# Sliding-window attention with a channel mix on one core: how batch 0's q and k come in, the bias matmuls, and the order of all five engines

## The chip, the core and the metric

The kernel runs on one core of a Trainium2 chip. A core has five engines with an instruction stream each: PE (TensorE, matmul), DVE (VectorE), ACT (ScalarE), POOL (GpSimd) and SP (SyncE, here only a queue of DMA issues). They work on SBUF and PSUM memory with 128 partitions and wait for each other on semaphores. DMAs are issued by SP and by POOL; in this kernel, POOL's also convert fp32 in DRAM to bf16 on the way, SP's don't. The metric is the device time of one execution in microseconds (us), as the median of several runs.

## What is computed

Inputs are q, k, v of 8 batches, 8 heads, 576 positions and head size 64, all fp32. The attention looks back over a window of 128 positions with a linear bias per head; its output, with the heads side by side (512 columns), is the input of a channel mix with a hidden size of 1024.

```
scores = scale * np.matmul(q, k.transpose(0, 1, 3, 2))
bias = slopes[:, None, None] * (-np.abs(rel).astype(np.float32))[None, :, :]
mask = (rel >= 0) & (rel < window)          # window = 128
scores = np.where(mask, scores + bias[None], -1000000000.0)
attn = softmax(scores)
x = matmul(attn, v)                         # heads side by side: [8, 576, 512]
x_prev = x shifted by one position
xk = mu_k * x + (1.0 - mu_k) * x_prev
xr = mu_r * x + (1.0 - mu_r) * x_prev
k = np.maximum(xk @ w_k, 0.0)
v = k * k @ w_v
r = 1.0 / (1.0 + np.exp(-(xr @ w_r)))
out = r * v
```

## The kernel before

**Tiles and stages.** The work of the attention is cut into 32 items: item `it` is batch `it // 4` and the pair `it % 4` of heads. The channel mix runs over 4 pairs of batches P (1152 rows), each cut into chunks of rows that begin at c0; `fo` counts the 8 blocks of the hidden size, and `c` the blocks of 128 rows of a pair. Every step is an op with a name, an engine, an estimate of its time and what it depends on:

- `lq`, `lql`, `lqp`, `lqn`: loads of q and k. `lq.g.i` (SP, `load_qk`, lines 111 to 114) brings fp32 of batch 0, pair g, i=0 for q and 1 for k. `lql.b.w.i` (POOL, `load_ql`, 136 to 140) brings half of the heads w of batch b as bf16. `lqp` (POOL, `load_qp`) does so for pair 1 of batch 0. `lqn.b.i.j` (POOL) brings batches 5 to 7 in another layout.
- `lts.b.i`: the last 64 positions ("tail") of q or k; `lvs.b.j`: block j of V; `lwk`, `lwr`, `lwv`: weights; all on POOL.
- `c.g.i`: cast of fp32 to bf16 with positions sorted (`cast_qk`); `ct.it`: the sorting copy alone for data that is bf16 already (`by_token`, DVE).
- `tq`, `tk`: 128x128 transposes of q and k on PE (`qk_transp`); `pq`, `pk`: copies of them from PSUM to SBUF (`qk_copy`). `tail.b`, `tcopy.b`: the same for the tails.
- `score.it.e`: half e of the scores of an item (`scores`, 196 to 230). For the items of batch 0 (`early`) it begins with two matmuls of 512 columns that write bias and mask into PSUM (lines 204 to 210). `exp.it.e`: the exponential on ACT; `mask.it.e`: multiplication with the mask on DVE for the other batches.
- `av.it`: attention times V; `norm.it`: division by the sum (DVE); `ot.it` and `xt.it`: transpose of the result and its copy; from item 12 on `xt` is a transposing DMA on SP. `xk.it`, `xr.it`: the two mixes (DVE).
- `m1` (and `m1a`, its first part for two blocks): xk times w_k; `rl`: relu on ACT; `kk`: its square; `m3`: xr times w_r; `rs`: tanh on ACT; `m2a`, `m2`: the two halves of kk times w_v; `oo`: the product (DVE); `st`: the store (SP).
- `tr.b.i`, `trt.b.i`: transposing DMAs on SP for q, k and tails of batches 5, 6, 7; `fill`, and `warm(8)` at the start: matmuls on zeros. `clear0`, `clear`, `ms`: memsets on POOL that V and `av` need.

**Where batch 0's q and k come from before.** Pair 0 comes as fp32 by two SP loads into the last `qt_buf` and is cast on DVE (`NHW = 1`). Pair 1 comes by two POOL loads (`lqp`), pairs 2 and 3 by two POOL loads (`lql.0.1.*`), as bf16, each followed by one `ct` per pair.

**What sets the order.** `plan()` (480 to 532) issues the ops, but the dictionary `ORDER` (743 to 888) gives, for each engine, the complete list, and each op waits until the one ahead of it in its list has been issued. So an engine executes its list strictly in turn: an op that waits holds up all that stand behind it on that engine. Buffers go around in rings: 2 PSUM buffers "sa" for scores (and `av` from batch 1 on), 4 PSUM buffers "mm" for everything else on PE, 3 "rl", 3 "ct" and so on; an op that takes a new buffer waits until the users of the one that is that many turns back are done.

**Which engine does what.** The engine of a `kk` is set by `KFO` and `KCH` (line 55): blocks 1 and 5 of eight chunks go to ACT (16 squares), the other 88 that are listed to DVE. `pq` and `xt` run on ACT, `pk`, `tcopy` and `c` on DVE.

Of the kernel before, what the change touches and what calls it, by code (L numbers as in the profile page):

```python
# [8 lines left out]
FP32 = mybir.dt.float32  # L9
# [7 lines left out]
def kernel(  # L17
# [59 lines left out]
    ldr = qt_buf[-1].rearrange("p i j g c -> p (i j g c)").bitcast(FP32)[  # L77
        :, 0:4 * NHW * NF * D].rearrange("p (i g h c) -> p i g h c", i=2, g=NHW, h=2)
# [32 lines left out]
    def load_qk(g, i):  # L111
        nc.sync.dma_start(
            out=ldr[:, i, g],
            in_=(q, k)[i][0, 2 * g:2 * g + 2, 0:SM].rearrange("h (p r) d -> p h (r d)", p=128))
# [47 lines left out]
    def qk_transp(it, t0, t1):  # L162
        cs = T["cs", it]
# [19 lines left out]
    def tail_copy(b):  # L183
        t4 = T.pop(("tt", b))[:, 0:128 * G].rearrange("p (g t c) -> p g t c", g=G, t=2)
        nc.vector.tensor_copy(out=tt_buf[b % 2][:, :, 0:3:2], in_=t4)
# [9 lines left out]

    def scores(it, e):
# [5 lines left out]
        w = sum(n for _, _, n in pieces)  # L202
        sa = T["sa", it, e] = p_sa.tile([128, 2, 512], FP32, tag="sa", name="sa")
        if early:
            for hl in range(2):
                nc.tensor.matmul(
                    sa[:, hl, 0:w] if e else sa[:, hl, 0:w].rearrange("p (u c) -> p u c", u=2),
                    lhsT=sid[:, 2 * g + hl],
                    rhs=dist if e else dist[:, None, 0:256].to_broadcast([128, 2, 256]),
                    start=True, stop=False, skip_group_check=True)  # L210
# [74 lines left out]
    def x_copy(it, c0=0, c1=S):  # L285
        b, g = divmod(it, G)
        nc.scalar.copy(out=xt_buf[b % 2][:, g, XO + c0:XO + c1], in_=T.pop(("xt", it, c0))[:, c0:c1])  # L287

    def x_scaled(it, c0, c1):
        if c0 == 0:  # L290
            T["xm", it] = mxp.tile([128, S], BF16, tag="xm", name="xm", bufs=3)
        nc.scalar.activation(out=T["xm", it][:, c0:c1], in_=xt_buf[0][:, it, XO + c0:XO + c1],
                             func=AF.Identity, scale=mu_sb[:, it:it + 1])
# [164 lines left out]
    def clear_first():  # L458
# [3 lines left out]
    RINGS = {"sa": 2, "mm": 4, "ct": 3, "xu": 3, "dl": 4, "xm": 3, "xk": 2, "rl": 3,  # L462
             "kk": 2, "rs": 6, "ot": 4}
# [567 lines left out]
```

## Time and profile before

| | us |
|---|---|
| median of 3 runs | 231.31 (231.19 to 232.16) |
| span of the profiled execution | 230.5 |
| PE busy | 222.2 |
| DVE busy | 192.2 |
| ACT busy | 155.4 |
| POOL busy | 88.7 |

The profiled execution is one run; its span goes from its first to its last instruction. Busy shares are averages over stages with different limits: the same engine can be the limit in the first 40 us and have time to spare later. Matmuls are pipelined, so that a busy PE need not be at its peak: a group of matmuls is better judged by the time until the next group begins, which the chain of work shows. How full the engines are along the span, the page shows in 40 slices of 5.8 us, a digit per slice, in tenths:

```profile
PE   7889899999999999999999999899999999999994
DVE  7577999999998998999798996996876998985252
ACT  4299999985999998783789555685168744226700
```

The DMA queues of the page:

```profile
q0 software_dynamic: 83600, 16.52, 92.3%
q1 hardware_dynamic: 33680, 16.79, 34.1%
```

q0 are the DMAs that POOL issues, q1 those of SP: packets, MB, and the time that their packets took as a share of 16 engines' span.

### The profile page before, as it was taken

To read this page: it belongs to the slowest core of one execution; us is meant where nothing else is said; L and a number is where in the kernel's file an instruction comes from. 1 tells how busy PE (TensorE), PEld (TensorE's weight loads), DVE (VectorE), ACT (ScalarE), POOL (GpSimd) and SP (SyncE) were. 2 spreads that over 40 slices of the span, in tenths; PEclk is the share of its full clock that TensorE was granted. 3 is DMA by queue.
4 is the path that set the end of the run, shared out by engine and by line. 5 is a ranking of instruction groups with operands and counts; after the bars stand their busy time and mean duration, and the time that the engine had idled before them with its cause. 6 is when DMAs were issued, how large, how long until landed. Compare 5 with 4: busy or idle time off the path is not lost.

```text
span 230.5 us, 5326 instructions
## 1 busy us (share of the span) xinstructions
PE 222.2 (96%) x2099; PEld 130.0 (56%) x2099; DVE 192.2 (83%) x409; ACT 155.4 (67%) x265; POOL 88.7 (38%) x127
## 2 busy tenths in 40 slices
PE   7889899999999999999999999899999999999994
PEld 2446577855685565456657554455574555456653
DVE  7577999999998998999798996996876998985252
ACT  4299999985999998783789555685168744226700
POOL 8987857563897000697001954540000000000000
PEclk9999999999999999999999999999999999999999
DMA  6999999999999986999996999999954252413014
GB/s 137 160 173 187 198 177 192 195 180 162 177 155 161 154 120 100 123 128 204 120 256 144 166 120 156 203 176 197 134 128 119 79 163 77 102 46 141 0 67 162
DMA packets 117305, 33.65 MB, mean 146 GB/s; under 512 B 99608, under 2 KB 112928, under 8 KB 117280
## 3 DMA queue, kind: packets, MB, share of 16 engines
q0 software_dynamic: 83600, 16.52, 92.3%
q1 hardware_dynamic: 33680, 16.79, 34.1%
q8 instruction: 16, 0.26, 0.4%
q14 instruction: 9, 0.07, 0.1%
HBM read 33.56 MB, written 9.44 MB: 187 GB/s over the span
## 4 chain that ended last, share of the span: by engine, by line
PE 84%; ACT 7%; DMA 4%; DVE 2%; issue 1%; SPq 0%; DVEq 0%
PE pv L364 25%; PE ps L326 25%; PE pr L349 13%; PE sa L262 7%; PE sa L229 6%; DMA tt<-ts 4%; PE wm L190 3%; PE tp L166 3%; ACT at L237 3%; ACT qk L146 2%; PE pv L371 2%; ACT xt L287 1%; PE tp L282 1%; DVE qk L143 1%; ACT rl L332 1%
## 5 line engine op out<-in xcount | busy, mean ns | idle before, releaser
L237 ACT ACTIVATE at<-sa 128x1024 bf16<-128x1024 f32 x64 | 64.7, 1043 | 14.3 <-PE sa L229 14.2
L326 PE MATMUL ps<-xk,wk_sb 128*128 128x256 bf16 (+2 forms) x416 | 73.2, 314 | 0.5 <-DVE xk L315 0.4
L332 ACT ACTIVATE rl<-ps 128x256 bf16<-128x256 f32 (+2 forms) x104 | 46.3, 482 | 37.0 <-PE ps L326 30.0
L364 PE MATMUL pv<-wv_sb,kk 128*128 128x512 bf16 x272 | 65.3, 379 | 0.0
L326 PEld LDWEIGHTS <-wk_sb 128*128 128x128 bf16 x416 | 38.5, 98 | 24.1 <-issue 2.4
L364 PEld LDWEIGHTS <-kk 128*128 128x128 bf16 x272 | 25.5, 98 | 28.4 <-issue 1.3
L246 DVE TENSOR_TENSOR at<-at,mask 128x1024 bf16<-128x1024 bf16 x56 | 37.4, 684 | 1.9 <-ACT at L237 1.9
L118 POOL DMA_DIRECT2D vs<-in_v_dram x32 | 28.5, 897 | 26.3 <-PE sa L262 16.1
L341 DVE TENSOR_TENSOR kk<-rl 128x256 bf16<-128x256 bf16 (+2 forms) x88 | 28.0, 335 | 10.3 <-ACT rl L332 10.1
L349 PE MATMUL pr<-wr_sb,xr 128*128 128x512 bf16 x144 | 36.0, 379 | 0.0
L379 DVE SCALAR_TENSOR_TENSOR ot<-rs,pv 128x512 f32<-128x512 bf16 (+1 forms) x38 | 24.4, 653 | 7.4 <-PE pv L364 5.8
L315 DVE SCALAR_TENSOR_TENSOR xk<-dl,mu_sb,xt 128x576 bf16<-128x576 bf16 (+2 forms) x36 | 27.1, 752 | 1.3
L315 DVE SCALAR_TENSOR_TENSOR xr<-dl,mu_sb,xt 128x576 bf16<-128x576 bf16 x32 | 25.5, 812 | 0.0
L355 ACT ACTIVATE rs<-pr 128x512 bf16<-128x512 f32 x36 | 21.5, 608 | 4.9 <-PE pr L349 4.6
L262 PEld LDWEIGHTS <-at 128*128 128x128 bf16 x576 | 21.6, 98 | 5.3 <-issue 0.4
L274 DVE TENSOR_TENSOR xu<-sa,rc 128x640 bf16<-128x640 f32 x28 | 23.1, 824 | 1.2 <-DMA xt<-xu 0.3
L146 ACT COPY qk<-tp 128x1024 bf16<-128x1024 bf16 (+1 forms) x20 | 18.9, 960 | 5.6 <-PE tp L166 4.6
L349 PEld LDWEIGHTS <-xr 128*128 128x128 bf16 x144 | 13.2, 98 | 12.6 <-issue 0.4
L90 POOL DMA_DIRECT2D ql<-in_k_dram x12 | 10.9, 919 | 23.0 <-DVE ct L157 21.1
L262 PE MATMUL sa<-vs,at 128*128 128x65 bf16 x448 | 18.9, 194 | 0.0
L308 DVE TENSOR_TENSOR dl<-xt 128x576 bf16<-128x576 bf16 (+2 forms) x36 | 15.1, 420 | 3.2 <-DMA xt<-xu 2.1
L229 PE MATMUL sa<-qk 64*128 64x256 bf16 (+1 forms) x160 | 13.2, 259 | 0.8 <-ACT qk L146 0.5
(70 smaller groups left out, 207.6 us busy)
## 6 DMA issues: line engine op xcount, KB each, us to landing
out_dram<-ot SPq DMA_DIRECT2D x34, 256.0 KB, 3.6
vs<-in_v_dram POOLq DMA_DIRECT2D x32, 128.0 KB, 8.0
ql<-in_k_dram POOLq DMA_DIRECT2D x9, 256.0 KB, 6.7
ql<-in_q_dram POOLq DMA_DIRECT2D x9, 256.0 KB, 7.3
ql<-in_k_dram POOLq DMA_DIRECT2D x13, 128.0 KB, 6.5
ql<-in_q_dram POOLq DMA_DIRECT2D x13, 128.0 KB, 7.6
wk_sb<-in_moe_w_k_dram POOLq DMA_DIRECT2D x2, 512.0 KB, 9.0
wv_sb<-in_moe_w_v_dram POOLq DMA_DIRECT2D x2, 512.0 KB, 8.5
```

The source lines that it names most:

```text
L118: nc.gpsimd.dma_start(out=vs_buf[b % NLD][:, j, :, 0:D], in_=v[b, :, 128 * j:128 * j + 128, :].rearrange("h p d -> p h d"))
L229: nc.tensor.matmul(to, lhsT=kk_, rhs=qq_, start=not early, stop=True, skip_group_check=True)
L237: nc.scalar.activation(out=at_half(it, e), in_=T.pop(("sa", it, e)), func=AF.Exp, scale=float(scale))
L246: nc.vector.tensor_tensor(out=at, in0=at, in1=m, op=ALU.mult)
L262: nc.tensor.matmul(pa[:, hl, W * (t - t0):W * (t - t0) + W], lhsT=at[:, lo:lo + 128], rhs=vs[:, u, 2 * g + hl, :] if u < NF else tvb[:, 2 ...
L315: nc.vector.scalar_tensor_tensor(out=to, in0=T["dl", it][:, c0:c1], scalar=mu_sb[:, NPO * which + g:NPO * which + g + 1], in1=xp, op0=ALU. ...
L326: nc.tensor.matmul(ps[:, 0:c1 - c0], lhsT=wk_sb[:, po, 128 * fo:128 * fo + 128], rhs=xk[:, po, c0:c1], start=(po == 0), stop=(po == NPO - 1))
L332: nc.scalar.activation(out=rl[:, 0:c1 - c0], in_=T.pop(("ps", P, c0, fo))[:, 0:c1 - c0], func=AF.Relu, scale=RELU_SCALE)
L341: nc.vector.tensor_tensor(out=T["kk", P, c0][:, fo, 0:c1 - c0], in0=rl[:, 0:c1 - c0], in1=rl[:, 0:c1 - c0], op=ALU.mult)
L349: nc.tensor.matmul(pr, lhsT=T["xr", P][:, po, 128 * c:128 * c + 128], rhs=wr_sb[:, po], start=(po == 0), stop=(po == NPO - 1))
L364: nc.tensor.matmul(pv, lhsT=kk[:, fo, o:o + 128], rhs=wv_sb[:, fo], start=(fo == 0), stop=(fo == NFO - 1))
L379: nc.vector.scalar_tensor_tensor(out=T["ot", P, c][:, w0:w1], in0=T["rs", P, c][:, w0:w1], scalar=1.0, in1=pv[:, 0:w1 - w0], op0=ALU.add, ...
```

## The change

1. **Loads.** `NHW = 4`: all four pairs of batch 0 come as plain fp32 by SP (eight `lq`), into both `qt_buf` (`ldr` is now a list over the two). `lqp` and `lql.0.*` are gone. The casts `c.g.i` write into `ql_buf[0]` (`cs0`), in the sorted order, so batch 0 has no `ct`. q and k of each pair have their own transposes `tq` and `tk` and their own copies `pq` and `pk`. `lql.2.*` now waits for the transposes of the pairs whose place it takes.
2. **Bias matmuls.** `scores` loses its first two matmuls for the early items; they are an op of their own, `bias.it.e`, which takes the "sa" buffer and depends on nothing but dist and sid.
3. **Engine by list.** `flex` makes an op that runs where the lists of `ORDER` put it, on ACT or on DVE: casts, `pq`, `pk`, `tcopy`, `xt` and, through `ENGOF`, `kk`. By the new lists 41 `kk` run on ACT (16 before); two of eight casts, `pk.0` and three `tcopy` on ACT; `pq.1`, `pq.2`, `pq.5` and `xt.8` on DVE.
4. **Order.** New lists for all five engines. `FILL` is (2, 2) instead of (5, 2, 3).
5. Code that no list used is removed (`XMUL`, `x_scaled`, rings "xm", "xk", "kk").

```diff
-    KFO, KCH = (1, 5), ((0, 512), (0, 768), (1, 0), (1, 512), (1, 896), (2, 0), (2, 512), (2, 896))
-    XMUL = ()
-    NHW = 1
+    NHW = 4
...
-    ldr = qt_buf[-1].rearrange("p i j g c -> p (i j g c)").bitcast(FP32)[
-        :, 0:4 * NHW * NF * D].rearrange("p (i g h c) -> p i g h c", i=2, g=NHW, h=2)
+    ldr = [t.rearrange("p i j g c -> p (i j g c)").bitcast(FP32).rearrange(
+        "p (g i h c) -> p g i h c", g=2, i=2, h=2) for t in qt_buf]
+    cs0 = ql_buf[0].rearrange("p w i h c -> p (w i h c)").rearrange(
+        "p (g i r h d) -> p g i r h d", g=G, i=2, r=NF, h=2)
...
     def cast_qk(g, i, f):
-        if i == 0:
-            T["cs", g] = csp.tile([128, 2, NF, 2, D], BF16, tag="ct", name="cs")
-        f(T["cs", g][:, i].rearrange("p r h d -> p h r d"),
-          ldr[:, i, g].rearrange("p h (r d) -> p h r d", d=D))
+        f(cs0[:, g, i].rearrange("p r h d -> p h r d"),
+          ldr[g // 2][:, g % 2, i].rearrange("p h (r d) -> p h r d", d=D))
...
+    def bias(it, e):
+        g = it % G
+        sa = T["sa", it, e] = p_sa.tile([128, 2, 512], FP32, tag="sa", name="sa")
+        for hl in range(2):
+            nc.tensor.matmul(
+                sa[:, hl] if e else sa[:, hl].rearrange("p (u c) -> p u c", u=2),
+                lhsT=sid[:, 2 * g + hl],
+                rhs=dist if e else dist[:, None, 0:256].to_broadcast([128, 2, 256]),
+                start=True, stop=False, skip_group_check=True)
...
     def square(P, c0, c1, fo):
         rl = T.pop(("rl", P, c0, fo))
-        if fo in KFO and (P, c0) in KCH:
+        if ENGOF.get(("kk", P, c0, fo)) == "ACT":
...
+    def flex(name, eng, busy, run, deps=(), pri=0, alloc=None, uses=()):
+        eng = ENGOF.get(name, eng)
+        f = {"ACT": act_cast, "DVE": vec_cast}[eng]
+        return op(name, eng, busy, lambda: run(f), deps, pri, alloc, uses)
...
+            if early:
+                op(("bias", it, h), "PE", 440, lambda h=h: bias(it, h), [("dcopy",), ("sid",)], n, "sa")
...
-    FILL = (5, 2, 3)
+    FILL = (2, 2)
```

The beginnings of the lists, before and after, as far as the prediction speaks of them ("..." where ops are left out):

```
PE before   fill.0 fill.2 tq.0 fill.1 tk.0 score.0.0 tmu tq.2 tq.3 score.2.0 score.3.0 tail.0
            tq.1 av.0.0 av.2.0 score.2.1 av.3.0 score.0.1 ... score.5.1 m1a.0.0.0 ot.1.1
            ot.3.1 m1.0.0.0 score.7.0 score.7.1 m1.0.0.7 ...
PE after    bias.0.0 tk.0 bias.3.0 tq.0 tk.3 tq.3 score.0.0 tq.2 score.3.0 tk.2 tail.0 fill.1
            bias.2.0 tk.1 score.2.0 tq.1 bias.1.0 av.0.0 av.3.0 tmu score.1.0 bias.2.1 ...
            ot.1.1 fill.0 m1a.0.0.0 m1.0.0.0 m1a.0.0.1 m1.0.0.1 tq.5 score.6.1 score.6.0 ...
ACT before  mask0.2 mask0.0 pq.0 exp.0.0 pq.2 mask0.4 pq.3 exp.2.0 exp.3.0 pq.1 mask0.6 exp.2.1
            exp.0.1 xt.2.0 xt.0.0 exp.1.0 xt.3.0 pq.4 exp.1.1 pq.5 exp.4.0 xt.1.0 exp.3.1 xt.0.1
            xt.2.1 exp.5.0 pq.7 exp.5.1 xt.1.1 xt.3.1 rl.0.0.0 ...
ACT after   mask0.2 mask0.6 mask0.0 mask0.4 c.2.1 pk.0 pq.0 pq.3 exp.0.0 exp.3.0 c.1.0 tcopy.0
            exp.2.0 exp.1.0 xt.0.0 exp.2.1 xt.3.0 xt.2.0 exp.0.1 pq.4 exp.3.1 xt.1.0 exp.1.1
            xt.2.1 xt.0.1 exp.4.0 pq.7 xt.3.1 pq.6 exp.7.0 xt.1.1 exp.4.1 rl.0.0.0 ...
DVE before  dcopy c.0.0 id8 c.0.1 sid pk.0 ct.2 ct.3 pk.2 cmu pk.3 ct.1 tcopy.0 pk.1 norm.2.0 ...
DVE after   id8 dcopy sid c.0.1 c.3.1 mcopy.1 c.0.0 c.3.0 mcopy.0 c.2.0 pk.3 c.1.1 pq.2 pk.2
            pk.1 pq.1 norm.0.0 norm.3.0 cmu norm.2.0 ...
POOL before lql.0.1.1 lql.0.1.0 clear0 lqp.1.1 lvs.0.0 lts.0.1 lqp.1.0 lts.0.0 lvs.0.1 lql.1.0.1
            ms lql.1.0.0 ... lwk.0 lwk.1 ... lqn.5.1.0 lqn.6.1.2 lqn.6.1.1 lvs.4.4 ... lqn.6.0.2
            lvs.5.1 lvs.5.2 lvs.5.0 lvs.5.3 lvs.7.1 ...
POOL after  clear lwk.1 lts.0.1 lts.0.0 ms clear0 lvs.0.0 lvs.0.1 lvs.0.4 lql.1.0.1 lql.1.0.0
            ... lts.1.0 lwk.0 ... lts.6.1 lqn.5.0.0 ... lts.5.1 lqn.6.0.0 lqn.5.1.3 lvs.5.4
            lqn.5.1.1 lts.6.0 lqn.6.1.0 lts.5.0 lqn.5.1.0 lvs.4.0 ... lqn.6.1.3 lvs.7.4 lvs.7.1
            lvs.5.2 lqn.6.0.2 lvs.5.0 lqn.6.0.1 lvs.5.1 ...
SP before   lq.0.0 lq.0.1 lmu.1 lmu.0 st.0.0 ... tr.6.1 tr.6.0 xt.17 ... xt.20 trt.6.0 trt.6.1 ...
SP after    lq.0.0 lq.0.1 lq.3.1 lq.2.1 lq.3.0 lq.2.0 lq.1.1 lq.1.0 lmu.1 lmu.0 st.0.0 ...
            tr.6.1 xt.16 st.0.6 trt.6.1 ... xt.18 st.1.0 trt.6.0 tr.6.0 xt.21 ...
```

The new PE list from the av of item 18 to the first scores of batch 6:

```
av.18 m2a.1.0 m2a.1.2 score.20.1 score.22.1 m2a.1.3 m2.1.0 score.22.0 score.23.0 m2.1.3 m2.1.2
m1.1.512.4 m1.1.512.2 m1.1.896.0 m3.1.4 m1.1.896.6 m3.1.5 m3.1.7 m1.1.512.5 m1.1.512.3 m1.1.896.1
m1.1.512.6 m1.1.512.7 m1.1.896.7 m1.1.896.2 m3.1.6 av.21 m1.1.896.4 m2a.1.6 m1.1.896.5 score.25.1
```

More of the change, by code (lines that the diff above doesn't have):

```diff
@@ L201, in scores @@
         a0 = BASE[pieces[0][0]] + pieces[0][1] - 128 * pieces[0][0]
-        w = sum(n for _, _, n in pieces)
-        sa = T["sa", it, e] = p_sa.tile([128, 2, 512], FP32, tag="sa", name="sa")
         if early:
[L205 to L210, printed above, removed]
+            sa = T["sa", it, e]
+        else:
+            sa = T["sa", it, e] = p_sa.tile([128, 2, 512], FP32, tag="sa", name="sa")
         for (u, q0, n) in pieces:
@@ L605, in add_pair @@
         for h in range(2):
-            op(("score", it, h), "PE", 760 if early else 330, lambda h=h: scores(it, h),
-               ready + (([("trt", b, 0), ("trt", b, 1)] if b in CROSSED else [("tcopy", b), ("clear0",)]) if h else []) + AVOF(it - NAT),
-               n, "sa")
+            if early:
+                op(("bias", it, h), "PE", 440, lambda h=h: bias(it, h), [("dcopy",), ("sid",)], n, "sa")
+            held = [("bias", it, h)] if early else []
+            op(("score", it, h), "PE", 330, lambda h=h: scores(it, h),
+               ready + (([("trt", b, 0), ("trt", b, 1)] if b in CROSSED else
+                         [("tcopy", b), ("clear0",)]) if h else []) + AVOF(it - NAT),
+               n, None if early else "sa", uses=held)
             op(("exp", it, h), "ACT", 920, lambda h=h: expo(it, h),
-               [], n, uses=[("score", it, h)])
+               [("score", it, h)], n, uses=[("bias" if early else "score", it, h)])
             got.append(("exp", it, h))
@@ L924, in add_qk @@
                [("tr", b - 2, 0), ("tr", b - 2, 1)] if b - 2 in CROSSED else
-               [("ct", G * (b - 2) + 2 * w + j) for j in range(2)]
-               if b > 2 or b == 2 and w else [], dma=dma[i], land=min(b, 2) * 700)
+               [("ct", G * (b - 2) + 2 * w + j) for j in range(2)] if b > 2 else
+               [(t, g) for t in ("tq", "tk") for g in range(2 * w, 2 * w + 2)] if b == 2 else [],
+               dma=dma[i], land=min(b, 2) * 700)
     def add_tails(b):
```

421 lines of the change are left out of this document (192 added, 229 removed).

## The prediction

> **What bounds the kernel now.** I read the page's busy line and slices first, then the table of stretches, then the order of time in the opening, then the waits.
>
> ```profile
> span 230.5 us, 5326 instructions
> PE 222.2 (96%) x2099; PEld 130.0 (56%) x2099; DVE 192.2 (83%) x409; ACT 155.4 (67%) x265; POOL 88.7 (38%) x127
> ...
> 0.00:10.00 10.00, 8.30 (x33) 3.28 (x33) 5.78 (x21) 3.47 (x7) 9.10 (x25) 1.00 1.09 150
> 10.00:20.00 10.00, 8.89 (x119) 5.28 (x120) 7.37 (x21) 9.05 (x17) 8.24 (x13) 1.00 1.91 167
> 20.00:30.00 10.00, 8.85 (x138) 6.45 (x135) 9.55 (x28) 10.00 (x16) 8.58 (x16) 1.00 1.37 201
> 30.00:40.00 10.00, 9.90 (x114) 7.36 (x112) 9.96 (x26) 9.81 (x21) 6.29 (x9) 1.00 1.80 182
> 40.00:60.00 20.00, 20.00 (x227) 12.65 (x225) 19.72 (x41) 16.00 (x26) 11.35 (x15) 1.00 1.92 188
> ```
>
> Columns of the stretches: length, then busy time of PE, PEld, DVE, ACT and POOL, the granted clock, DMA share, GB/s. From 40 us on PE is busy all the time, and the change leaves its matmuls there as they are. So PE's order of work can win only (a) in the opening, where PE has gaps, and (b) in single waits later. In the opening ACT (9.05, 10.00, 9.81) sets the pace, with DVE close behind it; before 10 us both are half idle.
>
> ```profile
> 13.62 0.40 PE L179 MATMUL to<-ident,ts 128*128 128x128 bf16 x4
> 14.30 0.53 PE L262 MATMUL pa<-vs,at 128*128 128x65 bf16 x12
> 16.34 1.93 ACT L237 ACTIVATE at<-sa 128x1024 bf16<-128x1024 f32 x2
> ...
> 28.75 0.49 ACT L332 ACTIVATE rl<-ps 128x256 bf16<-128x256 f32 x1
> ...
> 47.62 3.45 PE pv L364 x16
> ...
> PE sa L229 <- DMA tt<-ts: 0.8, 1, 0.8
> ```
>
> The landmarks (start, duration): tail.0 at 13.62, the first av at 14.30, exp.2.1 at 16.34, the first relu at 28.75, and, from the chain, m2a.0.0 at 47.62. The last row is the one later wait of PE of any size: 0.8 us on a DMA transpose of tails.
>
> **The change part by part.**
>
> *Loads of batch 0.* SP now issues eight plain loads instead of two, and the kernel casts each once.
>
> ```profile
> 0.74 0.45 SPq L112 DMA_DIRECT2D qt<-in_q_dram  x1
> 1.25 0.45 SPq L112 DMA_DIRECT2D qt<-in_k_dram  x1
> ...
> qt<-in_q_dram SPq DMA_DIRECT2D x1, 256.0 KB, 2.8
> qt<-in_k_dram SPq DMA_DIRECT2D x1, 256.0 KB, 3.1
> ...
> L143 DVE CAST cs<-qt 128x512 bf16<-128x512 f32 x2 | 1.4, 692 | 0.6 <-DMA qt<-in_q_dram 0.6
> L157 DVE COPY ct<-ql 128x1024 bf16<-128x1024 bf16 x19 | 9.0, 481 | 0.1
> ```
>
> The two landed at 0.74+2.8 = 3.5 and 1.25+3.1 = 4.35: one per 0.8 us. Eight in a row end at 3.5+7×0.8 = 9.1. The casts cost 8×0.69 = 5.5 instead of 2×0.69+3×0.48 = 2.8, so +2.7 us over DVE and ACT, nearly all before 12 us. In the first 20 us DVE stands idle for 6.9 and ACT for 7.5, mostly early; that hides them, so I take 0. Without that cover they cost 1.4 us, half on each engine. The fewer warm-up matmuls (12 instead of 18) cost or give nothing in work: PE has nothing else there.
>
> *POOL's queue.* It loses four issues of q and k, but its list now begins with clear (memsets of buffers 1 and 2), then lwk.1, and only then the tails and V of batch 0.
>
> ```profile
> 19.88 0.65 POOL L454 MEMSET tv<- 64x520 bf16 x1
> ...
> 21.61 0.39 POOL L904 MEMSET tt<- 128x256 bf16 x1
> ...
> 7.03 0.72 POOL L132 DMA_DIRECT2D ts<-in_q_dram  x1
> 7.72 0.91 POOL L118 DMA_DIRECT2D vs<-in_v_dram  x1
> ...
> 9.34 0.46 POOL L908 MEMSET at<- 128x64 bf16 x4
> 9.68 0.48 POOL L910 MEMSET xt<- 128x8 bf16 x2
> ...
> ts<-in_q_dram POOLq DMA_DIRECT2D x8, 64.0 KB, 6.4
> vs<-in_v_dram POOLq DMA_DIRECT2D x32, 128.0 KB, 8.0
> wk_sb<-in_moe_w_k_dram POOLq DMA_DIRECT2D x2, 512.0 KB, 9.0
> ```
>
> clear took 19.88 to 22.0, so 2.1 us. From 1.2 us on (where POOL has made dist) that gives: clear to 3.3, lwk.1 issued at 3.3, the two tail loads until 5.5, ms (9.34 to 10.16, 0.8) and clear0 (half of clear, 1.05) to 7.4, lvs.0.0 to 8.3, and lvs.0.1 issued at 8.3, where it was issued at 7.72. lwk.1 lands about 9.0 later, at 12.3, and the tails lie behind it in the same queue. If the tails don't feel it, lts.0.0 (issued at 4.8) lands at 4.8+6.4 = 11.2; if they do, at some 12.8. I take 12.4, since 512 KB at the 167 to 201 GB/s of the stretches fill 2.6 to 3.1 us. V is ready at 8.3+6.6 = 14.9 by the way from issue to use that lvs.0.1 had (7.72 to 14.30).
>
> [...]
>
> *The path of the opening.*
>
> ```profile
> 116.57 0.54 PE sa L229 x8
> 117.11 0.97 PE pv L364 x4
> 118.08 0.86 PE pr L349 x4
> ```
>
> From the chain: two halves of scores pass in 0.54, and four matmuls of 512 columns in 0.86. PE's new list holds tail.0, fill.1, bias.2.0, tk.1, score.2.0, tq.1, bias.1.0, av.0.0, av.3.0, tmu, score.1.0 in this order, so PE stops at tail.0 until 12.4. Behind it: two warm matmuls 0.43 (half of 0.86), bias 0.43, four transposes 0.25 (an estimate from the 0.40 with its tail at 13.62), scores 0.4, transposes 0.25, bias 0.43 come to 14.6. The two av's then run at 14.9 to 15.5, score.1.0 behind pq.1 at 15.7, and exp.1.0 starts at 16.2. From there until the first relu ACT's new list holds 8 exponentials, 8 xt copies and 3 pq of 1024 columns. From exp.2.1 at 16.34 the old list holds the same 8, 8 and 3, and took 28.75−16.34 = 12.4 us without a gap. So the first relu comes at 28.6: **the earlier q and k are eaten by the wait for tails and V, −0.15 us.** Bounds: 15.0 for exp.1.0 with both loads early, 17.4 with both late, so −1.3 to +1.1.
>
> *Squares and copies on the other engine.*
>
> ```profile
> L146 ACT COPY qk<-tp 128x1024 bf16<-128x1024 bf16 x16 | 16.5, 1054 | 0.7 <-PE tp L166 0.7
> L338 ACT ACTIVATE kk<-rl 128x256 bf16<-128x256 bf16 x6 | 2.6, 426 | 0.0
> L185 DVE COPY tt<-to 128x512 bf16<-128x512 bf16 x5 | 2.1, 416 | 1.3 <-PE to L179 1.3
> ```
>
> ACT gets 41 squares instead of 16. Five lie in the first two chunks, where ACT is the pace: 5×0.426 = 2.1, and tcopy.2 0.4 more, while pq.5 (1.05) goes to DVE: +1.5 us on ACT before m2a.0.0. ACT is idle for 4.0 of the 20 us from 40 on, so half of it may be hidden: I take +0.8 (0 to +1.5). The other twenty fall where PE never waits; ACT is idle for a third of the whole span: 0. DVE gets 25 squares fewer, which PE can't use when it is full.
>
> *Order later.* trt.6.0 and trt.6.1 now come up in SP's list well before the first scores that use them, so the wait of 0.8 goes: −0.8 (0 to −0.8). PE's list has 30 separate runs of scores behind the first m1 where it had 29; one run costs 0.2 by the rows above: four matmuls of 512 columns take 0.97 behind scores and 0.86 otherwise, and about as much is lost going in. At the end the same two halves of two row blocks remain; st.3.6 is now queued behind st.3.8: 0 (−0.2 to +0.5).
>
> **Sum:** −0.15 + 0.8 − 0.8 + 0.2 = +0.05 us on the profiled span of 230.5. The median of the runs, 231.31, is 0.8 above the span, so 231.4.
>
> **The rivals.**
>
> *The two crossed batches arrive late (slower).* POOL's list now has lvs.7.4 and lvs.7.1 ahead of lqn.6.0.2 and lqn.6.0.1; those V loads wait for the last av of batch 4 (av.18). Today nothing of batch 6 stands behind that wait:
>
> ```profile
> POOL vs L118 <- PE sa L262: 16.1, 1, 16.1
> ...
> ql<-in_q_dram POOLq DMA_DIRECT2D x13, 128.0 KB, 7.6
> ...
> DMA to landing us min/median/max: 4.3/5.2/8.8
> ```
>
> (The last row is that of the transposing DMAs at L95.) lqn.6.0.1 is issued some 4.3 us behind av.18 (0.7 + 4×0.9), lands 7.6 later, and tr.6.0 takes 5.2: 17.1. PE has, from av.18 to score.25.1, eleven groups of four by 512 columns (0.86), six by 384 (0.65), seven by 256 (0.43), two pairs of scores (0.54), one av (0.53) and two changes to scores (0.2): 18.4 us. So 1.3 us in hand at the medians, and a stall of 2.3 with 8.8 for the transpose. It decides from 6.5 us for the transpose on, or 8.9 for the load. tr.5.1 stands likewise behind lqn.6.0.0, which waits for ct.16. With a stall of 1.9: 231.4+1.9 = 233.3. Chance 0.20.
>
> *The clock falls (slower).*
>
> ```profile
> 1.19 6.44 PE L190 MATMUL wm<-zero 128*128 128x512 bf16 x16 [1.19 <-DVE zero L448]
> ...
> 7.70 0.59 PE L190 MATMUL wm<-zero 128*128 128x512 bf16 x2
> ```
>
> Sixteen matmuls of 512 columns take 0.40 each here, four take 0.86 later on, 0.215 each, and two at 7.70 already go in 0.59 with the last one's tail; the granted clock of the stretches stands at 1.00 throughout. So PE starts at half pace and leaves it by 7.7. [...] Chance 0.06. Tails and V at their late ends with all of ACT's extra time unhidden (+1.25+0.7 = 1.95) make 233.3, chance 0.06.
>
> *The opening does come earlier (faster).* Tails and V land as if lwk.1 and the plain loads weren't there, and the lighter DVE lets ACT's squares hide: −1.3 instead of −0.15, 0 instead of +0.8: 231.4 − 1.15 − 0.8 = 229.4. For it speaks that ACT is idle for 6.5 of the first 10 us and that masks, casts and two exponentials are moved there; against it, that PE's list stops at tail.0. Chance 0.31.
>
> **How the numbers follow.** Forecast 231.4 (230.2 to 232.5), chance 0.37. Faster 0.31 (229.4). Slower 0.20+0.06+0.06 = 0.32 (233.3 to 233.6). Half a per cent, 1.15 us, is about what a measurement of this kernel can tell from no change. The range reaches from 229.0, a little below the fast case, to 234.3, the slow case with the longer transpose.
>
> **What would show it.** In the changed kernel: tail.0 near 12.4, the first av near 14.9, exp.1.0 near 16.2, the first relu near 28.6, m2a.0.0 near 48.3; no row of PE waiting for tt<-ts. A row of PE L229 waiting for DMA qt<-ql would be the first rival; matmuls 0.4 apart behind 10 us the second; the first relu before 27.5 the third. The sum is wrong if PE's busy time from 60 us on is no longer full.

## The result and the profile after

The changed kernel takes 244.24 us (median of 4 runs, 243.18 to 244.72) where the kernel before took 231.3: a ratio of 1.055 [1.052, 1.059]. The forecast was 231.4 with a range up to 234.3. The change makes the kernel 13 us slower; the prediction, which expected no change that a measurement could tell, was wrong. The ratios here and below leave out executions that ran in a slower state than the others of the same kernel (so that of d_both leaves out 238.30 and isn't that of its median).

The page's span, busy line, and its slices of PE and of the granted clock:

```profile
span 242.2 us, 5302 instructions
PE 224.1 (92%) x2062; PEld 132.0 (55%) x2093; DVE 188.2 (78%) x385; ACT 164.6 (68%) x292; POOL 86.4 (36%) x123
...
PE   8659999999999999999999199999999999999994
...
PEclk9858999999999999999999769999999999999999
```

PE's busy time is nearly what it was (222.2 before), but the span is 11.7 us longer. (The medians differ by 12.9. Wherever both are on record, the time of an execution is 1.7 to 2.1 us above its span, so the execution profiled before was most likely its slowest, 232.16.) Two places stand out: the slices before 24 us, and one slice near 135 us in which PE is nearly idle. In both the granted clock falls too, which it did nowhere before (1.000 over its whole span). The table of stretches (length, busy PE, PEld, DVE, ACT, POOL, clock, DMA share, GB/s) says the same, and the waits of PE name the releasers:

```profile
10.00:20.00 10.00, 6.71 (x46) 3.74 (x47) 3.87 (x8) 4.00 (x5) 7.34 (x11) 0.51 1.98 173
120.00:140.00 20.00, 14.18 (x107) 8.63 (x108) 13.16 (x26) 9.34 (x22) 15.24 (x18) 0.91 2.19 156
...
PE sa L227 <- DMA qt<-ql: 6.1, 2, 5.7
PE to L172 <- DMA ts<-in_q_dram: 2.9, 1, 2.9
```

(In the wait rows: us in total, times, longest.) In the kernel before, PE was busy for all 20.00 us of the second stretch. First the opening, in the order of time, with the last tail load from the chain (issue, us to landing) ahead of it:

```profile
5.08 9.38 DMA ts<-in_q_dram
...
12.43 0.62 ACT L141 CAST ql<-qt 128x512 bf16<-128x512 f32 x1 [0.19 <-DMA qt<-in_q_dram]
14.59 0.58 PE L172 MATMUL to<-ident,ts 128*128 128x128 bf16 x4 [2.88 <-DMA ts<-in_q_dram]
15.21 0.58 ACT L141 COPY tt<-to 128x512 bf16<-128x512 bf16 x1 [2.17 <-PE to L172]
20.67 1.02 ACT L235 ACTIVATE at<-sa 128x1024 bf16<-128x1024 f32 x1 [1.76 <-PE sa L227]
33.26 0.72 ACT L318 ACTIVATE rl<-ps 128x256 bf16<-128x256 f32 x2
51.47 1.89 PE L350 MATMUL pv<-wv_sb,kk 128*128 128x512 bf16 x8
```

The rows behind the load are the last cast of batch 0, tail.0 (at 13.62 before), tcopy.0, exp.1.0, the first relu (28.75 before) and m2a.0.0. The last stood at 47.45 before by this same view (47.62 by the chain):

```profile
47.45 3.62 PE L364 MATMUL pv<-wv_sb,kk 128*128 128x512 bf16 x16
```

So **the opening costs 4.0 us**. Two things lie in it: tails that land late, and a clock at half from 10.2 to 20.5 us.

Then the place near 135 us. These are rows of POOL, SP and PE, and the time from issue to landing of the one transposing load tr.6.0 (last row):

```profile
114.83 0.69 POOL L122 DMA_DIRECT2D tv<-in_v_dram  x1 [20.79 <-PE sa L260]
...
118.97 0.92 POOL L90 DMA_DIRECT2D ql<-in_q_dram  x1
127.02 5.51 SPq L95 DMA_TRANSPOSE qt<-ql  x1
132.24 0.60 PE L312 MATMUL ps<-xk,wk_sb 128*128 128x256 bf16 x4
138.55 0.50 PE L227 MATMUL sa<-qt 64*128 64x256 bf16 x4 [5.71 <-DMA qt<-ql]
139.52 4.64 PE L350 MATMUL pv<-wv_sb,kk 128*128 128x512 bf16 x12
...
qt<-ql SPq DMA_TRANSPOSE x1, 11.4
```

POOL stood for 20.8 us at lvs.7.4 until av.18 was done, with lqn.6.0.2 and lqn.6.0.1 behind it. lqn.6.0.1 went out at 118.97 and landed 8.0 us later, so tr.6.0 was issued only at 127.02, took 11.4 us, and PE waited 5.7. The 12 matmuls behind that wait took 4.64 us (2.76 at full clock, in b_gate below): half clock again.

### The profile page after: what moved, and what is told of

It is laid out like the page before. It is cut to its first block, busy times and chain, and to the rows that moved or that the text cites. A ratio compares the mean times of both kernels' runs of the same rounds, so it can differ in the third digit from the quotient of the medians.

```text
span 242.2 us, 5302 instructions
## 1 busy us (share of the span) xinstructions
PE 224.1 (92%) x2062; PEld 132.0 (55%) x2093; DVE 188.2 (78%) x385; ACT 164.6 (68%) x292; POOL 86.4 (36%) x123
## 4 chain that ended last, share of the span: by engine, by line
PE 57%; DMA 15%; DVE 10%; POOL 8%; ACT 6%; issue 3%; POOLq 0%; ACTq 0%
PE pv L350 18%; PE ps L312 15%; PE pr L335 9%; DMA qt<-ql 7%; PE sa L227 5%; PE sa L260 4%; DMA ts<-in_q_dram 4%; POOL ql L90 3%; DVE at L244 3%; DMA ql<-in_k_dram 2%; ACT at L235 2%; POOL vs L118 2%; PE tp L159 2%; ACT rl L318 2%; DVE xu L272 2%
## 5 line engine op out<-in xcount | busy, mean ns | idle before, releaser
L235 ACT ACTIVATE at<-sa 128x1024 bf16<-128x1024 f32 x64 | 67.7, 1084 | 22.0 <-PE sa L227 21.9
L312 PE MATMUL ps<-xk,wk_sb 128*128 128x256 bf16 (+2 forms) x412 | 71.4, 313 | 0.3
L350 PE MATMUL pv<-wv_sb,kk 128*128 128x512 bf16 x258 | 66.0, 388 | 1.1 <-issue 0.5
L318 ACT ACTIVATE rl<-ps 128x256 bf16<-128x256 f32 (+2 forms) x104 | 47.8, 502 | 25.3 <-PE ps L312 24.6
L350 PEld LDWEIGHTS <-kk 128*128 128x128 bf16 x272 | 25.8, 100 | 28.8 <-issue 3.9
L335 PE MATMUL pr<-wr_sb,xr 128*128 128x512 bf16 x134 | 35.2, 379 | 0.5
L341 ACT ACTIVATE rs<-pr 128x512 bf16<-128x512 f32 x36 | 22.0, 635 | 13.3 <-PE pr L335 12.8
L327 DVE TENSOR_TENSOR kk<-rl 128x256 bf16<-128x256 bf16 (+2 forms) x63 | 19.9, 332 | 14.1 <-ACT rl L318 14.1
L324 ACT ACTIVATE kk<-rl 128x256 bf16<-128x256 bf16 (+2 forms) x41 | 21.2, 537 | 0.1
L335 PEld LDWEIGHTS <-xr 128*128 128x128 bf16 x144 | 13.6, 98 | 13.1 <-issue 0.4
L141 ACT COPY qk<-tp 128x1024 bf16<-128x1024 bf16 (+1 forms) x18 | 17.8, 1003 | 0.7 <-PE tp L159 0.4
L227 PE MATMUL sa<-qk 64*128 64x256 bf16 (+1 forms) x160 | 13.8, 269 | 0.9 <-ACT at L235 0.4
```

The lines of the kernel that those rows point to most:

```text
L227: nc.tensor.matmul(to, lhsT=kk_, rhs=qq_, start=not early, stop=True, skip_group_check=True)
L235: nc.scalar.activation(out=at_half(it, e), in_=T.pop(("sa", it, e)), func=AF.Exp, scale=float(scale))
L312: nc.tensor.matmul(ps[:, 0:c1 - c0], lhsT=wk_sb[:, po, 128 * fo:128 * fo + 128], rhs=xk[:, po, c0:c1], start=(po == 0), stop=(po == NPO - 1))
L318: nc.scalar.activation(out=rl[:, 0:c1 - c0], in_=T.pop(("ps", P, c0, fo))[:, 0:c1 - c0], func=AF.Relu, scale=RELU_SCALE)
L335: nc.tensor.matmul(pr, lhsT=T["xr", P][:, po, 128 * c:128 * c + 128], rhs=wr_sb[:, po], start=(po == 0), stop=(po == NPO - 1))
L350: nc.tensor.matmul(pv, lhsT=kk[:, fo, o:o + 128], rhs=wv_sb[:, fo], start=(fo == 0), stop=(fo == NFO - 1))
```

## The experiments

Fifteen kernels were run. All change the kernel after the change, and the kernel before was run again beside each set (231.1 to 231.6). "m2a.0.0" is where the first group at L350 starts in the profile, before: 47.5; "half clock" is how long the clock was at half in the first 24 us of that profile, from the first record of the clock on (at 6.83 us in the changed kernel).

| run | us, median (range) | ratio to before | m2a.0.0 | half clock |
|---|---|---|---|---|
| after | 244.24 (243.18 to 244.72) | 1.055 [1.052, 1.059] | 51.5 | 10.2 |
| a_mid | 243.51 (242.16 to 244.70) | 1.053 [1.048, 1.058] | 51.4 | 6.8 |
| a_open | 244.13 (242.96 to 245.30) | 1.056 [1.052, 1.061] | 48.8 | 6.8 |
| a_both | 242.94 (241.02 to 244.10) | 1.050 [1.043, 1.057] | 47.9 | 6.8 |
| a_warm | 242.84 (240.99 to 244.46) | 1.050 [1.043, 1.057] | 48.5 | 0 |
| b_gate | 239.61 (238.61 to 239.82) | 1.035 [1.031, 1.039] | 50.6 | 6.8 |
| b_cross | 239.92 (238.95 to 240.47) | 1.037 [1.032, 1.041] | 50.9 | 10.2 |
| b_hot | 245.14 (241.03 to 245.81) | none | 50.3 | 6.8 |
| b_all | 238.78 (237.90 to 240.56) | 1.033 [1.027, 1.039] | 48.9 | 0 |
| c_gate_open | 238.42 (237.46 to 240.49) | 1.032 [1.026, 1.039] | 47.6 | 0 |
| c_spread | 240.49 (240.05 to 241.30) | 1.039 [1.034, 1.045] | 52.5 | 10.2 |
| c_spread_open | 237.21 (236.34 to 238.04) | 1.026 [1.020, 1.031] | 47.9 | 0 |
| c_bias | 244.36 (240.41 to 244.82) | none | 50.4 | 6.8 |
| d_ot | 237.63 (236.93 to 237.79) | 1.026 [1.019, 1.033] | 48.6 | 0 |
| d_tr5 | 238.40 (237.66 to 239.40) | 1.030 [1.024, 1.037] | 49.4 | 3.4 |
| d_both | 237.17 (234.56 to 238.30) | 1.018 [1.007, 1.028] | 49.4 | 3.4 |

b_hot and c_bias have no ratio: three of the four executions of each took 244.2 to 245.8, about as long as the changed kernel, and one 241.0 and 240.4, so no verdict rests on their times.

**First set: take away each late issue.** The theory was that lvs.7.4 and lvs.7.1 hold up lqn.6.0.1, and that lwk.1 ahead of the tails makes the opening late; the rival was that the clock alone does the latter.

```diff
 a_mid, POOL:   lqn.6.1.3 [-lvs.7.4 lvs.7.1-] lvs.5.2 lqn.6.0.2 lvs.5.0 lqn.6.0.1 lvs.5.1 [+lvs.7.4 lvs.7.1+]
 a_open, POOL:  [-clear lwk.1-] lts.0.1 lts.0.0 ms clear0 lvs.0.0 lvs.0.1 [+clear lwk.1+] lvs.0.4
 a_both:        both
 a_warm, PE:    [+3 zero matmuls+] tq.0 ... [+2+] tq.2 ... [+12+] tail.0
```

a_mid:

> The changed kernel with two issues moved on POOL's list: lvs.7.4 and lvs.7.1, which wait for av.18, go behind lvs.5.1, so lqn.6.0.2 and lqn.6.0.1 no longer stand behind that wait. Theory (order of POOL's list): tr.6.0 lands before PE asks for it, the wait of 5.7 us of PE on qt<-ql at 132.8 falls below 1 us, the clock stays full there (it was at half for 6.8 us, 136.5 to 143.4, worth about 2.2 us of matmuls), so 244.2 - 5.7 - 2.2 = 236.3. Rival (the queue of POOL's loads is full whatever their order, the transpose is slow because of it): the wait only shrinks to 3 us or moves, 240 or more.

a_open:

> The changed kernel with clear and lwk.1 moved on POOL's list from its beginning to behind lvs.0.1: tails and V of batch 0 are issued first. Theory (the opening waits for the tails): tail.0 runs before 10 us instead of 14.6, the clock doesn't fall between 10 and 20 us, the fourth exponential of batch 0 starts near 15.5 instead of 20.7, the first relu near 28.5 instead of 33.3, total 244.2 - 4.5 = 239.7. Rival (the opening is bound by the work on ACT and DVE, which has grown by casts and squares): tail.0 earlier but the first relu not before 32, total above 242.5.

a_both:

> Both moves of the two runs before. Theory: the two losses add up, 244.2 - 7.9 - 4.5 = 231.8, level with the kernel before the change. If they share a cause (the load on the DMA engines, or the clock), less than their sum: 234 or more.

a_warm:

> The changed kernel with 17 more matmuls on zeros in PE's list where PE waits in the opening: 3 ahead of tq.0, 2 ahead of tq.2, 12 ahead of tail.0. Nothing else moves, and the tails land when they did. Theory (the clock is a loss of its own): granted clock 1.00 instead of 0.51 from 10 to 20 us, tail.0 still at 14.6, the fourth exponential at 18.5 instead of 20.7, total 244.2 - 2.0 = 242.2. Rival (PE only waits there, so its pace costs nothing): clock 1.00 but total within 0.7 of 244.2.

Measured: 243.5, 244.1, 242.9 and 242.8. In a_open, a_both and a_warm the opening gave back 2.7 to 3.6 us at m2a.0.0, but of the end next to nothing came. In a_open tail.0 came at 12.87 instead of 14.59, where under 10 was expected, and what the opening gained was lost again at tr.6.0. It was issued at 127.23, no earlier than in the changed kernel, and PE, which got there sooner, waited 8.2 us for it instead of 5.7:

```profile
PE sa L227 <- DMA qt<-ql: 9.6, 2, 8.2
```

In a_mid lqn.6.0.1 was issued at 96.0 instead of 118.97, and still the time hardly moved. Its rows show why. tr.5.1 on SP, the last four of the five POOL loads that now stand ahead of POOL's wait (the first was issued at 93.40), PE's first scores that need tr.5.1, and the landing of tr.6.0:

```profile
93.60 4.45 SPq L95 DMA_TRANSPOSE qt<-ql  x1
...
94.26 0.91 POOL L90 DMA_DIRECT2D ql<-in_q_dram  x1
95.13 0.92 POOL L118 DMA_DIRECT2D vs<-in_v_dram  x1
96.00 0.93 POOL L90 DMA_DIRECT2D ql<-in_q_dram  x1
96.86 0.94 POOL L118 DMA_DIRECT2D vs<-in_v_dram  x1
...
104.79 0.61 PE L227 MATMUL sa<-qt 64*128 64x256 bf16 x4 [4.85 <-DMA qt<-ql]
...
qt<-ql SPq DMA_TRANSPOSE x1, 12.7
```

The same two steps in the changed kernel:

```profile
94.37 4.05 SPq L95 DMA_TRANSPOSE qt<-ql  x1
100.50 0.39 PE L227 MATMUL sa<-qt 64*128 64x256 bf16 x4 [0.36 <-DMA qt<-ql]
```

From the issue of tr.5.1 to the scores that use it passed 6.1 us; with one more load of POOL issued just ahead of it and four just behind it, 11.2. PE lost 4.85 us there instead. And tr.6.0 was not earlier at all: issued at 127.58, since on SP's queue it stands behind stores and xt's of items that were now late, and it took 12.7 us (the last row of a_mid). So the simple theory fell, and a new one for this kernel came out of it: **a transposing load is slow (11.2 us here from issue to use, against 6.1) when POOL's converting loads are in flight beside it, also those issued after it.** a_warm says of the opening that the half clock was the larger part of it, since the tails are as late there: from tcopy.0 to exp.1.0 it takes 3.06 us by these rows, where the rows of the changed kernel give 20.67−15.21 = 5.46.

```profile
10.00:20.00 10.00, 9.30 (x95) 5.27 (x97) 6.02 (x17) 5.77 (x9) 7.58 (x11) 1.00 1.94 177
...
14.83 0.59 ACT L141 COPY tt<-to 128x512 bf16<-128x512 bf16 x1 [1.62 <-PE to L172]
17.89 1.02 ACT L235 ACTIVATE at<-sa 128x1024 bf16<-128x1024 f32 x1 [0.62 <-PE sa L227]
```

**Second set: the loads beside the transposing load.**

```diff
+    def gate_pool(b, i):
+        nc.gpsimd.memset(qn_buf[b % 2][:, i, 0, 0:2], 0.0)
+    op(("gp", b, i), "POOL", 60, ..., [("tr", b, i)])
 b_gate, POOL:   lqn.6.0.1 lvs.5.1 [+gp.6.0+] lvs.6.3 ...
 b_cross, POOL:  lqn.6.1.3 [+gp.5.1 lqn.6.0.2 lqn.6.0.1+] lvs.7.4 lvs.7.1 lvs.5.2 lvs.5.0 lvs.5.1 ...
          SP:    tr.6.1 [+tr.6.0+] xt.16 ...
 b_hot, PE:      [+24 zero matmuls+] score.25.1
 b_all:          b_cross + a_open + a_warm
```

The memset overwrites two columns of what the transposing load reads, so it waits until that load is done, and POOL's queue with it: in b_gate that queue started 711 packets from 125 to 132 us, in the changed kernel 4622 from 125 to 130.

b_gate:

> Edit: a 2-element memset on POOL that overwrites part of what tr.6.0 reads, put behind lvs.5.1, so that the 17 loads behind it start only when tr.6.0 has landed. Nothing is issued earlier: tr.6.0 still starts at 127.0. Theory (a transposing load is slow because POOL's casting loads that are issued beside and behind it share the DMA engines): tr.6.0 takes 5 to 6.5 us as tr.5.1 did (94.4 to 100.4) instead of 11.4, TensorE's wait of 5.7 us shrinks to under 1.5, and the half clock behind it goes: 244.2 - 4.5 - 2.5 = 237. Rival (it is slow because of its own size or because the loads ahead of it are what it waits for): it takes 11 us as before, 244.

b_cross:

> Edit: POOL's lqn.6.0.2 and lqn.6.0.1 in front of lvs.7.4, but held by a 2-element memset until tr.5.1 has landed, and tr.6.0 on SP's queue right behind tr.6.1. Theory (loads beside the transposing load, and a late start): tr.5.1 keeps its 6 us (TensorE's wait at 100 stays at 0.5, against the 5.0 that a_mid had), tr.6.0 starts near 108 and lands before 116, no wait at 132 and no half clock behind it: 244.2 - 5.7 - 2.5 = 236. Rival (the order itself loses the time, the waits only show it): another wait of 4 us or more comes up behind score.25, 240 to 244.

b_hot:

> Edit: 24 zero matmuls (about 5.2 us) in TensorE's list right ahead of score.25.1, where it waits 5.7 us for tr.6.0. The wait stays as long as it is in the changed kernel, but is filled with work that nobody needs. Theory (a wait of this length drops the granted clock to half for the 7 us behind it, and that costs by itself): the clock stays 1.0 through 136 to 144 and the time is 244.2 - 2.5 = 241.7. Rival (the half clock costs nothing, since other engines lag in that stretch anyhow): 244 to 244.7.

b_all:

> Edit: b_cross, with a_open's POOL list (lwk.1 and its memsets behind lvs.0.1) and a_warm's 17 zero matmuls in the opening. Theory (opening, clock and the two transposing loads are all that the change lost): first gated matmul (m2a.0.0) at 47 to 48 as before the change, no wait over 1 us behind it, 231 to 232. Rival (the new lists are slower by themselves, with ACT full from 30 to 80): 235 or more without a wait over 2 us.

Measured: 239.6, 239.9, (245.1), 238.8. b_gate is the sharpest of all: nothing was moved ahead, 17 loads were put off, and 4.6 us of the time went (in the two profiles 0.9 of it lies in the opening, which nobody touched, and 3.8 behind m2a.0.0). Its landing row for tr.6.0, and PE's scores that need it with the 12 matmuls behind them:

```profile
qt<-ql SPq DMA_TRANSPOSE x1, 4.3
...
131.73 0.34 PE L227 MATMUL sa<-qt 64*128 64x256 bf16 x4
...
132.28 2.76 PE L350 MATMUL pv<-wv_sb,kk 128*128 128x512 bf16 x12
```

4.3 us instead of 11.4, no wait, full clock: the theory stands and its rival falls, as far as the size of the transfer and the loads up to lvs.5.1 go. In the changed kernel six of the 17 loads went out ahead of tr.6.0 (119.8 to 125.6) and the others behind it; the gate holds back both, so it doesn't tell which of them slow it. b_cross agrees: tr.6.0 early and with few loads beside it (no packet of POOL's queue in the 0.1 us around its issue near 109.4) took 4.3, too. But both stayed 3 us above what was expected. In b_gate the loads that were put off meet the xt transposes instead:

```profile
xt<-xu SPq DMA_TRANSPOSE x1, 8.9
...
154.61 0.46 DVE L299 TENSOR_TENSOR dl<-xt 128x576 bf16<-128x576 bf16 x1 [2.28 <-DMA xt<-xu]
...
155.98 0.82 PE L312 MATMUL ps<-xk,wk_sb 128*128 128x384 bf16 x4 [1.35 <-DVE xk L301]
```

(The first row is the xt issued at 145.65; in the changed kernel the median of such transfers is 2.8 us, and the longest, 7.5, was issued at 132.62, beside loads of POOL's as well.) PE loses 2.2 of the 20 us from 140 on, where the changed kernel loses 0.1, and the clock stands at half for 3.4 us behind that. b_hot could not say what half clock costs: besides the two levels of its times, its 5.3 us of zero matmuls ran out and a wait of 2.77 us was left, behind which the clock fell all the same.

In b_all the clock stays full to the end (1.000 over the span) and no single wait of PE is over 1.2 us, yet the time is 238.8, not 232. In its profile m2a.0.0 comes 1.5 later than before, and from there to the end it takes 187.0 where the kernel before takes 183.1. That fits its rival, that about 4 us lie in the lists themselves, without showing where.

**Third set: add the parts up, and undo one part of the change.**

```diff
 c_gate_open:    b_gate + a_open, with 6 zero matmuls ahead of tq.0 and 3 ahead of tq.2
 c_spread, SP:   trt.5.1 [+tr.6.1 tr.6.0+] st.0.7 ...
          POOL:  lqn.6.1.3 [+gp.5.1 lqn.6.0.2 lqn.6.0.1 gp.6.0+] lvs.5.2 lvs.5.0 lvs.5.1 ... lvs.6.2 [+lvs.7.4 lvs.7.1+]
 c_spread_open:  c_spread + the opening of c_gate_open
 c_bias, PE:     each bias.it.e right ahead of its score.it.e
```

c_gate_open:

> Edit: b_gate with the opening mended too: POOL's lwk.1 and the long memsets behind lvs.0.1, and 9 zero matmuls (6 ahead of tq.0, 3 ahead of tq.2) to hold the clock. Theory (the opening costs about 3 us, once no later wait absorbs it): m2a.0.0 at 47 to 48 instead of b_gate's 50.6, time 239.6 - 3 = 236.6. Rival (what the opening gains is waited away behind the gate, as it was in a_open and a_both): 239 to 240 with m2a.0.0 early.

c_spread:

> Edit: the changed kernel's opening as it is; tr.6.1 and tr.6.0 on SP's queue right behind trt.5.1; on POOL a gate until tr.5.1 has landed, then lqn.6.0.2 and lqn.6.0.1, a gate until tr.6.0 has landed, then the other loads from about 111 instead of 131. Theory (transposing loads and POOL's casting loads slow each other wherever they meet; b_gate only moved the meeting to xt.22 and xt.20, whose 8 to 9 us delay the mixes at 155): the loads run out before 130, xt's that DVE and TensorE wait for behind 145 take 2.5 to 5 us, TensorE loses under 1.5 us between 100 and 165 and the time is 239.6 - 2.5 = 237. Rival (the lists are bound by ACT and DVE between 95 and 165, not by transfers): 239 to 240 with waits on rl, kk or ot in place of those on xt.

c_spread_open:

> Edit: c_spread and the opening of c_gate_open together. Theory (three places add up: opening 3, transposing load 4.6, its neighbours 2.5): 244.2 - 3 - 4.6 - 2.5 = 234, 3 above the kernel before the change. Rival (lists bound by ACT and DVE): 236.6.

c_bias:

> Edit: in the changed kernel each of the 8 bias entries moves back to right ahead of its score in TensorE's list, as it was inside score before. Theory (the split is worth little: TensorE waits for loads in the opening anyway): 244 to 245, m2a.0.0 within 0.7 us of 51.5. Rival (the split itself cost time, by holding the two sa buffers while others waited): 242 or less; rival to that (the split hid 0.86 us for each of four groups): 246 or more.

Measured: 238.4, 240.5, 237.2, (244.4). The opening is worth 3.3 us between c_spread and c_spread_open, whose intervals are apart; between b_gate and c_gate_open it is 1.2 us, within the intervals, though m2a.0.0 came 3.0 earlier: there tr.7 and an xt met POOL's put-off loads (a tr.7 took 9.6 us to land, and DVE waited 3.8 for an xt), and the rival (waited away behind the gate) is half right. c_spread didn't reach its 237, partly because its own opening was 1.9 later than b_gate's (52.5 and 50.6); from m2a.0.0 to the end both profiles take 186.9. So spreading the loads gained nothing that shows. c_bias moved m2a.0.0 by 1.1 us to the early side, no more than openings that nobody touched differ by (50.3 to 52.5 in six profiles), so the split of the bias is not shown to cost or to give anything.

**Fourth set: is the rest transfers?** In c_spread_open two waits on transfers were left, DVE's for stores and PE's for tr.5.1.

```diff
 d_ot:    otp.tile(..., name="ot", bufs=[-4-][+5+]), "ot": [-4-][+5+]
 d_tr5, POOL:  [+lqn.5.1.3 lqn.5.1.1 lqn.5.1.0+] lqn.6.0.0 lvs.5.4 lts.6.0 lqn.6.1.0 lts.5.0 lvs.4.0 ...
 d_both:  both
```

d_ot:

> Edit: c_spread_open with five output buffers (ot) instead of four. In c_spread_open VectorE waits 4.0 us in two places for a store to land before it may write the next output tile, and TensorE has nothing to do at 119.9 (1.5 us). Theory (the last 4 us are waits on transfers that the new order left no room for): that wait goes, 237.2 - 1.0 to 1.5 = 236. Rival (the order is bound by ACT and DVE as such there): 237.2, with the wait under another name.

d_tr5:

> Edit: c_spread_open with lqn.5.1.3, lqn.5.1.1 and lqn.5.1.0 in front of lqn.6.0.0 in POOL's list, five loads earlier, so that tr.5.1 can start near 87 instead of 90.9. Theory (transfers): TensorE's wait of 0.9 to 1.1 us at 97 for qt goes, and tt's at 106 with it: 236. Rival (ACT and DVE): 237.2.

d_both:

> Edit: both of these on c_spread_open. Theory (transfers): 234.5 to 235, still 3.5 above the kernel before the change, since smaller waits behind the mixes stay. Rival (ACT and DVE): 237.2. If it came to 232 or less, all of the loss would be transfers.

Measured: 237.6, 238.4 and 237.2, so nothing that can be told from c_spread_open. DVE's waits from 85 to 165 us, in c_spread_open:

```profile
DVE ot L365 <- DMA out_dram<-ot: 4.0, 2, 2.0
...
DVE dl L299 <- DMA xt<-xu: 2.0, 1, 2.0
```

And in d_ot:

```profile
DVE rc L271 <- PE sa L260: 4.8, 4, 1.5
DVE ot L365 <- PE pv L350: 3.9, 5, 2.0
DVE dl L299 <- DMA xt<-xu: 3.5, 1, 3.5
```

The wait for stores is gone, and others took its place. By the expectations as written this speaks for the rival, an order that is too late there whatever one transfer does. But the waits that came up are again in part for transfers, and two of the three openings were 1.5 us later than c_spread_open's. **What holds the rest of the loss stays open.** No version beats the kernel before; c_spread_open gives back 7 of the 13 us, and 6 are left. By the two profiled spans 4.1 are left, and of these PE's idle time shows 2.5: from 85 to 165 us PE stands idle for 3.3 in c_spread_open and for 0.8 in the kernel before.

## Why the prediction was wrong, step by step

- **Eight plain loads, one per 0.8 us, done at 9.1.** Wrong: the last cast waited for its load until 12.43. The estimate took its pace from two loads in the kernel before; here the later ones took 4.8 to 8.1 us to land, where those two took 2.8 and 3.1. That POOL's transfers beside them are the reason is only argued.
- **Tails at 12.4.** Wrong by 2.2 us: tail.0 at 14.59, beyond even the late end of 12.8. The load was issued at 5.08, near the 4.8 of the forecast, but took 9.4 us to land instead of 6.4.
- **From tail.0 to exp.1.0 in 3.8 us.** It took 6.1 (14.59 to 20.67), since that work ran at half clock. This is the second rival, the falling clock, with its price right (233.6−231.4 = 2.2; here 6.1−3.8 = 2.3) and its chance (0.06), the author's estimate, far too low. No run shows the 2.2 us as the price of PE's stop ahead of tail.0: the clock fell at 10.24, before that stop (11.71 to 14.59) and behind a window in which PE was busy for 1.72 of 3.41 us (its rows stand in the last section), and stayed at half for 10.2 us.
- **12.4 us of ACT from exp.1.0 to the first relu.** Right: 33.26−20.67 = 12.6.
- **ACT's extra squares, +0.8.** Too high: from the first relu to m2a.0.0 it took 18.2 us, and 18.7 before (47.45−28.75). They cost nothing that shows there.
- **The wait for trt goes, −0.8.** Right: no such row is left. The 0.2 for one more run of scores can't be told apart.
- **The crossed batch (first rival, 233.3, chance 0.20).** The mechanism was right in each step but one. lqn.6.0.1 was to be issued 4.3 us behind av.18; from POOL's first issue at 114.83 it was 4.1. From that first issue tr.6.0 came 12.2 us later (4.3+7.6 = 11.9 in the prediction). PE's cover was to be 18.4; from 114.83 to the end of its last work near 132.8 it was 18.0. **The term that failed is the duration of the transposing load: 5.2, at most 8.8, by a median over before, measured 11.4.** With it the sum gives 12.2+11.4−18.0 = 5.6, and the wait was 5.7. A median from stretches where POOL's queue was often quiet (in the kernel before it started no packet in the 5 us behind the issue of four of the six such loads, 507 and 1078 behind the other two) was used for a place where this same change puts a burst of loads around the transfer (5512 packets in the 5 us behind the issue of tr.6.0); b_gate, with 4.3 instead of 11.4 us, shows that the burst is the cause.
- **The rivals as alternatives.** The slow cases were given chances as if one of them at most would come. They came together: 4.0 in the opening, 5.7 at tr.6.0, and 2.3 for half clock behind it (from 138.55 to the next av at 144.00 is 5.45 us, the same groups in b_gate from 131.73 to 134.88, 3.15); less 0.8 for trt that is 11.2 of the 11.7 us of span. The range, drawn to single rivals, couldn't hold that sum (and its top, 234.3, is not the slow case with the longer transpose, which with the prediction's own stall of 2.3 is 233.7). The sum says where the trace loses time, not what mending returns: in a_open the opening gained 2.7 and the wait at tr.6.0 grew by 2.5, and in b_gate the wait and the half clock, 8.0 together, were gone and 3.8 came back behind m2a.0.0.
- **"PE's order can win only in the opening and in single waits later."** Right as far as winning goes, but it hid that a full PE can be lost: with the three places mended 4 us of span are left. Apart from the crossed batch and the wait for trt, the prediction put the new lists beyond the opening at +0.2; that term was too small (from m2a.0.0 to the end c_spread_open takes 186.7, the kernel before 183.1), and no run shows what makes up the rest.

What the runs show as cause: the loads beside tr.6.0 slow it (11.4 us, 4.3 in b_gate); the half clock is the larger part of what the opening loses (m2a.0.0 at 51.5, at 48.5 in a_warm, at 47.5 before); the opening as a whole is worth 3.3 us once tr.6.0 is mended (c_spread against c_spread_open). Only argued: that lwk.1 is what delays the tails; a_open, which moves it, recovers the opening but changes what else runs early, too.

## What to carry to other kernels

The same transposing load took from 4.3 to 13.6 us in these kernels: before using a median of a transfer's duration, look at what the other queue has in flight at that moment, and also at what will be issued behind it. When a wait is removed, ask which transfers now start together; a_mid and a_both took the wait at tr.6.0 down from 5.7 to 1.7 and 2.1 us and got one of 4.85 and 6.9 at tr.5.1. And slow cases that share a cause (loads bunched at one place) belong added up in the range, not weighed against each other.

## What the runs showed of the hardware that was not expected

**The clock fell behind a window in which PE was not idle.** In the changed kernel's trace it changed at 10.24, 20.48, 136.53 and 143.36 us, so that it stood at half for 10.24 and 6.83 us, three and two times 3.41. The four windows of 3.41 us up to its first recovery were:

```profile
6.83:10.24 3.41, 1.72 (x21) 1.04 (x20) 3.39 (x7) 2.69 (x5) 3.27 (x7) 1.00 1.05 255
10.24:13.65 3.41, 1.28 (x11) 0.47 (x8) 1.90 (x4) 2.16 (x3) 2.05 (x4) 0.50 1.76 191
13.65:17.07 3.42, 2.25 (x11) 1.36 (x12) 0.00 (x0) 0.58 (x1) 2.85 (x4) 0.50 2.27 149
17.07:20.48 3.41, 3.41 (x30) 1.85 (x27) 2.18 (x6) 1.02 (x1) 2.68 (x4) 0.50 1.93 176
```

(Second number: PE busy; the clock is the number after POOL's.) PE was busy for 1.72 of the 3.41 us, and the next window ran at half. The clock came back behind the window with 3.41 us, not behind the one with 2.25. The second time it fell behind a window without PE work (0.00 us from 133.12 to 136.53) and came back behind another full one (3.41 us from 139.95 to 143.36). In a_warm, whose zero matmuls keep PE busy for 2.40 and 3.19 us in two such windows of the opening, the clock stayed full:

```profile
7.37:10.78 3.41, 2.40 (x24) 1.25 (x26) 2.86 (x6) 2.88 (x5) 3.32 (x7) 1.00 1.15 239
10.78:14.19 3.41, 3.19 (x20) 1.31 (x16) 1.36 (x3) 1.64 (x2) 2.12 (x4) 1.00 2.09 170
```

How much PE work in a window holds the clock or brings it back, these windows don't show.

**The transposing load tr.6.0 took from 4.3 to 13.6 us** (b_gate, b_cross; a_both). In the 0.1 us around its issue POOL's queue started 8 packets in b_gate, none in b_cross and 105 in a_both. That loads issued behind a transposing load slow it, too, rests on a_mid, where four of the five loads that came to stand beside tr.5.1 were issued after it and 11.2 us passed from its issue to its use instead of 6.1. How the two queues share their turns, no run here shows.
